# Retention attention and a snake MLP on one Trainium2 core: blocks of one batch each with a ninth block of all ends, 64x64 state products, DMA turns, and another order for the first three blocks

## The chip, the cores and the metric

The kernel runs on one core of a Trainium2 chip. The metric is device time in microseconds: three timed runs gave 337.48, 338.91 and 339.41, median 338.91. Engines are called PE (TensorE), VectorE or DVE, ScalarE or ACT, POOL (GpSimd) and SP (SyncE, which issues most DMAs).

## The reference

Eight batches of eight heads, 576 tokens, head width 64. The attention has no softmax: scores are weighted with a decay by distance.

```
scores = (q @ k^T) / 8
ret    = scores * gamma[h] ** (i - j)   for i >= j, else 0
x      = (ret @ v) with heads side by side            # 4608 tokens x 512
h      = x @ w_in                                      # 512 -> 2048
g      = h + sin(alpha * h) ** 2 / (alpha + 1e-9)
out    = g @ w_out                                     # 2048 -> 512
```

## The kernel before

The 4608 tokens are projected in nine blocks of 512. For each block `gemm1(n, fc)` makes 16 products of four 128x512 matmuls (line 385) into a PSUM bank `hps`, ScalarE takes the sine (390), one of three engines squares it (399, 401), and VectorE adds h and the scaled square (406) into `gT`. `gemm2(n, u)` makes the second projection in 16 parts of four matmuls (421), four parts to a 128-token output `ops`, which ScalarE evicts (427) and SP stores (429). The projections take their input from `xT`, a ring of 2048 tokens; since a batch has 576 tokens and a block 512, a block straddles batches.

A batch's attention works on three parts: p = 0 and 1 are 256 tokens each, p = 2 the last 64 (the *ends*). Loads (110, 117) bring 512 KB per part and name; `cast` multiplies keys and queries with the decay, in two instructions of 512 elements (129), and copies values (149, 151); the operands are then *turned* (transposed), on PE by 64x64 products (206) with a copy back by ScalarE or VectorE (217, 219), or by a DMA (`crossed`, 183). `scores` multiplies keys and queries in 64x64 products (286), VectorE masks them (297). `outer` makes key-value sums of 128 tokens (231); `chain` on POOL (257, 269, 270), or for the first two batches VectorE (252), sums them up with decay into `state`, which holds each 64x64 state twice, half of it zeros, so that `add_states` can use full 128x128 products (352) on top of `values` (340). The sum goes to `xT` (363).

Each engine runs its own instructions in program order, and the order is written by hand: a prologue that computes batch 0 with filler matmuls (`keep_busy`, 455) in between, block 0's first projection, a stretch with batch 1 and half of block 0's second projection, then a loop over blocks in which lists (`at_unit`) place the next batch's attention between the 16 units of a block. A small DMA that reads w_out (`gate`, 517) holds back batch 1's loads until that slab has landed. Batches 0 to 3 are turned on PE, the others by DMA. PSUM has two double banks `mm`, three banks `hp` and one `op`.

Of the kernel before, what the change touches and what calls it, by code (L numbers as in the profile page):

```python
# [16 lines left out]
def kernel(  # L17
# [9 lines left out]
):  # L27
    nc = tc.nc
# [4 lines left out]
    P = 128  # L33
# [25 lines left out]
    ident_np = np.tile(np.eye(64, dtype=np.float16), (2, 1))  # L62

    ident_dram = nc.inline_tensor(ident_np, name="rt_ident")
# [8 lines left out]
    ident = const.tile([P, 64], F16, tag="ident", bufs=1)  # L73
# [3 lines left out]
    fac_s = {"k": cn[:, 32:36], "q": cn[:, 36:40]}  # L77
    g1 = cn[:, 40:44]
    g2 = cn[:, 44:52].rearrange("p (a t) -> p a t", t=2)
# [6 lines left out]
    RING = 2048  # L86
    xT = const.tile([P, KT, RING], F16, tag="xT", bufs=1)

    src = {"q": q, "k": k, "v": v}
    w_in_r = moe_w_in.rearrange("(Q t e d) f -> Q t d e f", Q=2, t=2, e=2)  # L90
    w_out_r = moe_w_out.rearrange("(a p) d -> p a d", p=P)

    def load_w_in(g):
        cols = slice(g * FF // 2, (g + 1) * FF // 2)
        for Q in range(2):
            for t in range(2):
                nc.gpsimd.dma_start(
                    w_in16[64 * t : 64 * t + 64, 2 * Q : 2 * Q + 2, cols], w_in_r[Q, t, :, :, cols]
                )
# [3 lines left out]

    raw = {}
    half = {}

    def load(b, nm, p):
        if p < 2:
            t_ = work.tile([P, H, 2 * D], F32, tag="raw", bufs=6, name=nm + "32")
            nc.sync.dma_start(  # L110
                t_, src[nm][b, :, 256 * p : 256 * p + 256, :].rearrange("h (i r) d -> i h (r d)", r=2)
            )
        else:
            t_ = work.tile([P, 4, D], F32, tag="raws", bufs=3, name=nm + "s32")
            view = src[nm][b, :, 512:576, :].rearrange("(hp e) i d -> e i hp d", e=2)
            for e in range(2):
                nc.sync.dma_start(t_[halves(e)], view[e])  # L117
        raw[b, nm, p] = t_
# [3 lines left out]
    def cast(b, nm, p, eng):  # L122
        t_ = raw.pop((b, nm, p))
        if p < 2:
            dst = work.tile([P, H, 2, D], F16, tag=nm + "16", bufs=nbuf[nm], name=nm + "16")
            if nm in fac:
                dst = dst.rearrange("p h r d -> p (h r d)").rearrange("p (a r t d) -> p a r t d", a=4, r=2, t=2)
                for A in range(2):
                    eng.tensor_tensor(  # L129
                        dst[:, 2 * A : 2 * A + 2].rearrange("p a r t d -> p t (a r) d"),  # L130
                        t_[:, 4 * A : 4 * A + 4].rearrange("p (t a) (r d) -> p t (a r) d", t=2, r=2),
                        fac[nm][:, 8 * A : 8 * A + 8]
                        .rearrange("p (t x) -> p t x", t=2)
                        .unsqueeze(3)
                        .to_broadcast([P, 2, 4, D]),
                        MULT,
                    )
                half[b, nm, p] = dst
                return
            d_ = dst.rearrange("p h r d -> p (h r) d")  # L140
            s_ = t_.rearrange("p h (r d) -> p (h r) d", r=2)
        else:
            d_ = dst = work.tile([P, 4, D], F16, tag=nm + "s16", bufs=3, name=nm + "s16")
            s_ = t_
            f_ = fac_s[nm].unsqueeze(2).to_broadcast([P, 4, D]) if nm in fac else None
        if nm != "v":
            eng.tensor_tensor(d_, s_, f_, MULT)
        elif eng is nc.scalar:
            eng.copy(d_, s_)
        else:  # L150
            eng.tensor_copy(d_, s_)  # L151
        half[b, nm, p] = dst

    def halves(n):
        return slice(64 * n, 64 * n + 64)

    def head_of(a, t):
        return 4 * (a // 2) + 2 * t + a % 2

    class Attention:  # L160
        def __init__(self, b):
            self.b = b
            self.c0 = b * S
            self.T = {}
            self.o = {}
            self.ret = {}
            self.sc = {}
            self.state = work.tile([P, 4, 4, 2, D], F16, tag="s16", bufs=2, name="s16")
            self.kvs = work.tile([P, 4, 4, D], F32, tag="kvs", bufs=1, name="kvs")

        def new_T(self, p):
            n = 8 if p < 2 else 2
            self.T[p] = [
                work.tile([P, n, P], F16, tag=nm + ("T" if p < 2 else "Ts"), bufs=3 if p < 2 else 2, name=nm + "T")
                for nm in "kq"
            ]

        def crossed(self, p):
            self.new_T(p)
            for w, nm in enumerate("kq"):  # L180
                x = half[self.b, nm, p]
                x = x.rearrange("p a r t d -> p (a r t d)") if p < 2 else x.rearrange("p h d -> p (h d)")
                nc.sync.dma_start_transpose(self.T[p][w], x)

        def transposes(self, p, nms="kq"):
            W = 512 if p < 2 else 128
            if p not in self.T:
                self.tr = psum.tile([P, 2, 1024], F16, tag="mm", bufs=2, name="tr")
                self.new_T(p)
            tr = self.tr  # L190
            for nm in nms:
                w = "kq".index(nm) * W
                x = half[self.b, nm, p]
                todo = []
                if p < 2:
                    for a in range(4):
                        for r in range(2):
                            todo.append([(t, g, x[halves(g), a, r, t, :], w + 128 * a + 64 * r)
                                         for t in range(2) for g in range(2)])
                else:  # L200
                    for Q in range(2):
                        todo.append([(t, g, x[halves(g), 2 * Q + t, :], w + 64 * Q)
                                     for t in range(2) for g in range(2)])
                for n, four in enumerate(todo):
                    for t, g, x_, col in four:
                        nc.tensor.matmul(  # L206
                            tr[halves(t), g, col : col + 64], x_, ident[halves(g), :],
                            start=(n == 0), stop=(n == len(todo) - 1), is_transpose=True, skip_group_check=True,
                        )

        def take(self, p, nm, eng):
            W = 512 if p < 2 else 128
            w = "kq".index(nm)
            s_ = self.tr[:, :, w * W : w * W + W].rearrange("p g (x i) -> p g x i", i=64)
            d_ = self.T[p][w].rearrange("p x (g i) -> p g x i", g=2)
            if eng is nc.scalar:
                eng.copy(d_, s_)  # L217
            else:
                eng.tensor_copy(d_, s_)  # L219

        def outer(self, ps, spare=False):
            if spare:
# [4 lines left out]
            todo = [(x, a, r) for x in range(len(ps)) for a in range(4) for r in range(2)]  # L227
            for n, (x, a, r) in enumerate(todo):
                for t in range(2):
                    for g in range(2):  # L230
                        nc.tensor.matmul(
                            kv[g][halves(t), 256 * x + 64 * a : 256 * x + 64 * a + 64],
                            half[self.b, "k", ps[x]][halves(g), a, r, t, :],
                            half[self.b, "v", ps[x]][halves(g), head_of(a, t), r, :],
                            start=(n == 0), stop=(n == len(todo) - 1), skip_group_check=True,
                        )
            N = len(ps)
            if spare:
                self.kv = kv
            else:  # L240
                nc.scalar.copy(  # L241
                    self.kvs[:, 2 * ps[0] : 2 * ps[0] + 2 * N].rearrange("p (x g) a d -> p g x (a d)", g=2),
                    kv2[:, :, 0 : 256 * N].rearrange("p g (x y) -> p g x y", x=N),
                )
# [163 lines left out]
    def rows_of(G):  # L408
        b, l = divmod(G, 9)
        if l == 8:  # L410
            return out[576 * b + 512 : 576 * b + 576, :]
# [318 lines left out]
```

## Time and profile before

| what | us |
|---|---|
| median of the runs | 338.91 |
| profiled execution, first to last instruction | 335.8 |
| last matmul ends, last copy 0.59, last stores land | 331.1 to 335.8 |
| PE / DVE / ACT / POOL busy | 311.6 / 232.5 / 170.0 / 153.9 |
| units of four 128x512 matmuls done by 64.8 / by 95.6 / in all | 24 / 48 / 288 |
| PE on one batch's ends in a steady block (scores 0.16, values 0.17, states 0.11) | 0.44 |
| ScalarE: copy of 1024 elements / sine / square / output copy | 1.01 / 0.69 / 0.63 / 0.59 |
| VectorE: four sums of L252 / inva, two instructions | 0.85 / 0.42 |
| POOL: 512 elements scaled / 1024 copied / 256 elements | 1.1 / 1.12 / 0.72 |
| DMA turn, from issue to landing | 3.3 to 3.4 |
| PE at 25.50 | first product of the first projection |

Busy times overlap across engines; a modelled matmul counts past the start of the next one, so PE's pace is read from the distance of starts. In the table by stage, a stage with PE near its length is full, the others wait. In the chain of waits each piece names who set the end there.

### The profile page before, as it was taken

Reading aid. Unit: us, or ns where it says so; the run is one execution under the profiler, and the core shown is the slowest. Engines: PE = TensorE matmul, PEld = TensorE weight load, DVE = VectorE, ACT = ScalarE, POOL = GpSimd, SP = SyncE. Lnnn points to the kernel's source line nnn. Section 1 sums busy time; section 2 is a strip of 40 time slices with the busy share of each in tenths; the row PEclk is TensorE's granted clock in tenths of the full one; section 3 lists DMA queues with packets and bytes.
Section 4 is the critical chain, followed back from the end, with each engine's and each line's share of the span. In section 5 each row is a group of like instructions: output and inputs, shape, how many; then the busy total and the mean of one; then the engine's idle time right before and its main releaser. Section 6 shows DMA issues by size and latency. Waiting matters only on the chain.

```text
span 335.8 us, 8508 instructions
## 1 busy us (share of the span) xinstructions
PE 311.6 (93%) x3561; PEld 150.2 (45%) x3561; DVE 232.5 (69%) x354; ACT 170.0 (51%) x257; POOL 153.9 (46%) x175
## 2 busy tenths in 40 slices
PE   7879947799889999999999999999999999999994
PEld 2344424444445444444444544544454444444441
DVE  3745953674849976978799779878965666666600
ACT  2427935378675563555455545554564454445411
POOL 0861380694793995499149906990720000000000
PEclk9989995999999999999999999999999999999998
DMA  8999989996242768993869487947111112111142
GB/s 217 260 205 205 262 223 286 204 234 169 57 123 71 194 158 169 183 273 94 180 166 266 104 158 189 279 94 150 41 33 31 34 31 56 38 33 31 32 94 63
DMA packets 93511, 47.77 MB, mean 142 GB/s; under 512 B 36496, under 2 KB 87840, under 8 KB 93472
## 3 DMA queue, kind: packets, MB, share of 16 engines
q1 hardware_dynamic: 89712, 42.89, 54.0%
q0 software_dynamic: 3264, 4.20, 7.1%
q8 instruction: 28, 0.46, 0.6%
q10 hardware_dynamic: 496, 0.13, 0.2%
q14 instruction: 11, 0.09, 0.1%
HBM read 37.23 MB, written 9.44 MB: 139 GB/s over the span
## 4 chain that ended last, share of the span: by engine, by line
PE 66%; POOL 9%; DVE 8%; ACT 5%; DMA 5%; issue 3%; SPq 2%; ACTq 1%; POOLq 0%
PE ops L421 30%; PE hps L385 27%; DVE ret L297 3%; PE o L340 3%; POOL s L257 2%; PE o L352 2%; DMA qT<-q 2%; ACT s_t L390 2%; PE sc L286 2%; DVE gT L406 2%; DMA eye<-rt_eye 2%; SPq L117 1%; DMA k<-in_k_dram 1%; POOL kvs L270 1%; POOL k L129 1%
## 5 line engine op out<-in xcount | busy, mean ns | idle before, releaser
L390 ACT ACTIVATE s_t<-hps,alpha_t 128x512 f16<-128x512 f32 x144 | 98.6, 687 | 110.6 <-PE hps L385 106.2
L385 PE MATMUL hps<-xT,w_in 128*128 128x512 f16 x576 | 145.7, 380 | 3.6 <-DVE gT L406 2.5
L421 PE MATMUL ops<-w_out,gT 128*128 128x512 f16 x576 | 146.2, 381 | 0.0
L406 DVE SCALAR_TENSOR_TENSOR gT<-ss_t,inva,hps 128x512 f16<-128x512 f16 x144 | 106.9, 747 | 12.0 <-ACT ss_t L399 7.5
L401 DVE TENSOR_TENSOR ss_t<-s_t 128x512 f16<-128x512 f16 x124 | 71.8, 579 | 45.9 <-ACT s_t L390 45.4
L385 PEld LDWEIGHTS <-w_in 128*128 128x128 f16 x576 | 56.4, 98 | 71.7 <-issue 5.6
L421 PEld LDWEIGHTS <-gT 128*128 128x128 f16 x576 | 53.4, 98 | 60.2 <-issue 0.8
L257 POOL TENSOR_TENSOR s<-kvs,cn 128x512 f16<-128x512 f32 x32 | 35.9, 1122 | 59.8 <-ACT kvs L241 46.5
L297 DVE TENSOR_TENSOR ret<-sc,mask 128x1024 f16<-128x1024 f32 x32 | 38.5, 1219 | 9.1 <-PE sc L286 8.5
L427 ACT COPY osb<-ops 128x512 f32<-128x512 f32 x36 | 21.1, 587 | 19.4 <-PE ops L421 19.4
L129 POOL TENSOR_TENSOR q<-q,cn 128x512 f16<-128x512 f32 x26 | 28.0, 1094 | 0.0
L129 POOL TENSOR_TENSOR k<-k,cn 128x512 f16<-128x512 f32 x24 | 26.3, 1113 | 2.3 <-DMA k<-in_k_dram 2.3
L363 ACT CAST xT<-o 128x1024 f16<-128x1024 f32 x14 | 14.2, 1012 | 10.3 <-PE o L352 10.3
L151 POOL CAST v<-v 128x1024 f16<-128x1024 f32 x13 | 14.6, 1122 | 8.6 <-DMA v<-in_v_dram 8.6
L270 POOL TENSOR_TENSOR kvs<-s,kvs 128x256 f32<-128x256 f32 x19 | 14.1, 742 | 7.5 <-ACT kvs L241 6.1
L286 PE MATMUL sc<-qT,kT 64*64 64x128 f16 x512 | 12.2, 220 | 3.0 <-DVE qT L219 1.3
L455 PE MATMUL idle<-zero 128*128 128x512 f16 x40 | 13.3, 469 | 1.2 <-DVE zero L450 1.2
L340 PE MATMUL o<-ret,v 64*64 64x128 f16 x512 | 11.1, 226 | 3.0 <-issue 1.8
L217 ACT COPY kT<-tr 128x1024 f16<-128x1024 f16 (+1 forms) x12 | 9.6, 797 | 8.5 <-PE tr L206 8.4
L269 POOL TENSOR_TENSOR s<-kvs,cn 128x256 f32<-128x256 f32 x19 | 13.6, 717 | 0.0
L286 PEld LDWEIGHTS <-kT 64*64 64x64 f16 x512 | 8.7, 106 | 10.8 <-issue 10.4
L340 PEld LDWEIGHTS <-v 64*64 64x64 f16 x512 | 8.3, 111 | 8.8 <-issue 8.7
(50 smaller groups left out, 136.5 us busy)
## 6 DMA issues: line engine op xcount, KB each, us to landing
out_dram<-osb SPq DMA_DIRECT2D x72, 128.0 KB, 2.4
k<-in_k_dram SPq DMA_DIRECT2D x16, 512.0 KB, 5.8
q<-in_q_dram SPq DMA_DIRECT2D x16, 512.0 KB, 6.7
v<-in_v_dram SPq DMA_DIRECT2D x16, 512.0 KB, 7.0
w_in<-in_moe_w_in_dram POOLq DMA_DIRECT2D x8, 256.0 KB, 9.8
w_out<-in_moe_w_out_dram POOLq DMA_DIRECT2D x4, 512.0 KB, 13.9
ks<-in_k_dram SPq DMA_DIRECT2D x18, 64.0 KB, 4.3
qs<-in_q_dram SPq DMA_DIRECT2D x18, 64.0 KB, 3.4
```

The source lines that it names most:

```text
L129: eng.tensor_tensor(dst[:, 2 * A : 2 * A + 2].rearrange("p a r t d -> p t (a r) d"), t_[:, 4 * A : 4 * A + 4].rearrange("p (t a) (r d) -> ...
L257: nc.gpsimd.tensor_tensor(self.state[:, n], self.kvs[:, n].unsqueeze(2).to_broadcast([P, 4, 2, D]), g2.unsqueeze(3).to_broadcast([P, 4, 2, ...
L270: nc.gpsimd.tensor_tensor(kvs[:, n], s32, kvs[:, n], ADD)
L286: nc.tensor.matmul(sc[halves(g), t, x : x + 128], T[0][halves(t), 2 * a + r, halves(g)], T[1][halves(t), 2 * a : 2 * a + 2, halves(g)], st ...
L297: nc.vector.tensor_tensor(ret.rearrange("p t (z x) -> p (t z) x", z=2), sc.rearrange("p t (z x) -> p (t z) x", z=2), mask[:, 0:256].unsque ...
L340: nc.tensor.matmul(o[halves(t), g, N * a : N * a + N], x, y, start=(n == 0), stop=False, skip_group_check=True,)
L385: nc.tensor.matmul(hps, w_in16[:, a, fc * P : (fc + 1) * P], xT[:, a, bs0 : bs0 + 512], start=(a == 0), stop=(a == KT - 1),)
L390: nc.scalar.activation(s_t, hps, mybir.ActivationFunctionType.Sin, bias=0.0, scale=alpha_t[:, fc : fc + 1],)
L401: eng.tensor_tensor(ss_t, s_t, s_t, MULT)
L406: nc.vector.scalar_tensor_tensor(gT[n][:, fc, :], ss_t, inva[:, fc : fc + 1], hps, MULT, ADD)
L421: nc.tensor.matmul(o, gT[n][:, fk, c * P : (c + 1) * P], w_out16[:, fk, :], start=(fk == 0), stop=(fk == FC - 1),)
L427: nc.scalar.copy(osb, o)
```

## The change

Blocks 0 to 7 are now the first 512 tokens of one batch each (`xT` is a tile per batch), and block 8 holds the eight ends (`xS`): the ends of two batches share the 128 partitions in one tile, their keys and queries are turned by DMA only, and the class `Ends` computes two such pairs at once during block 7. States are stored once (`state` for three chunks, `sS` for the last of each batch), and `add_states` uses 64x64 products like the rest. `values` comes in two calls, by `same`: first the products whose row half of the array adds into the other bank of the pair, then those that add into their own, with a drain of PE (`change_rows`) between. Casts are one instruction of 1024 elements, or two halves on two engines. On PE a turn is a 128x128 product (`turn`), one operand at a time, for batches 0 and 1 alone; batches 2 and 3 now go by DMA. w_in comes in four slabs of 512 columns, w_out's first slab opens the gate.

The order of blocks 0 to 2 is new: 19 filler matmuls instead of 40; block 0's first four units and block 1's first three are done in halves of 256 tokens, the first halves ahead of the rest; batch 1 runs beside all of block 0's second projection; batch 2 is computed within block 1 and batch 3 within block 2, one block ahead as in the loop. POOL casts batches 2 and 3 during block 1.

```
-            for n, (g, x, c, a) in enumerate(todo):
-                nc.tensor.matmul(
-                    self.o[p][:, g, N * x : N * x + N],
-                    self.state[:, c, a].rearrange("p t d -> p (t d)"),
...
+    def change_rows():
+        nc.tensor.drain()
...
+        def values(self, p, same):
+            for x in range(2):
+                for r in range(2):
+                    for e in range(2):
+                        for g in range(2):
+                            t = g if same else 1 - g
...
+                            matmul(
+                                o[halves(e), t, c : c + 128],
+                                v16[halves(g), 4 * t + 2 * x + e, r, :],
+                                self.ret[p, x][halves(g), t, m : m + 128],
...
+        def add_states(self, p, gs=(0, 1)):
...
+                            matmul(
+                                o[halves(e), t, c : c + 128],
+                                st[halves(t), a, :],
+                                qT[halves(t), 2 * a : 2 * a + 2, halves(g)],
...
+    def turn(b, nm, p, ys=(0, 1), tag="hp"):
...
+                matmul(
+                    tr[:, 256 * a + 128 * r : 256 * a + 128 * r + 128],
+                    x[:, a, r].rearrange("p t d -> p (t d)"),
+                    ident,
...
-        loads(0, (0, 1, 2))
+        for nm, p in ("k0", "q0", "k1", "q1", "v0", "v1"):
+            load(0, nm, int(p))
...
-        nc.sync.dma_start(gate, w_out16[:, 4, 0:64])
-        loads(1, (0,))
-        loads(0, (2,))
-        loads(1, (1,))
+        nc.sync.dma_start(gate, w_out16[:, 0, 0:64])
+        for nm, p in ("k0", "q0", "k1", "q1", "v0", "v1"):
+            load(1, nm, int(p))
...
+        for u in range(4):
+            project(0, u, 0, TAGS[u])
...
+        firsts(0, 4, TAGS, "GVGAGVGAGVGAGVGA", 1, {
+            8: [lambda: second(0)],
+            12: [lambda: second(1)],
+            15: [lambda: second(2), lambda: refill("k", 0, V)],
+            17: [lambda: refill("q", 0, V)],
+        })
+        second(4, 5)
+        turn(1, "k", 0)
+        take(1, "k", 0, A_)
+        second(3)
+        refill("k", 1, V)
+        second(6)
+        turn(1, "q", 0)
+        take(1, "q", 0, A_)
+        refill("q", 1, G_)
+        second(7)
+        turn(1, "k", 1)
+        take(1, "k", 1, V)
+        A.scores(0, 0)
+        A.scores(0, 1)
...
+        second(11)
+        change_rows()
+        A.values(0, True)
+        A.add_states(0)
+        A.outer((1,))
...
+        firsts(1, 3, TAGS, "VAVAVAVAVAVAVAVA", 0, todo)
+        gemm2(1, 3)
+        gemm2(1, 4)
+        A.values(1, False)
+        change_rows()
+        A.values(0, True)
+        A.add_states(0)
...
+            if A:
+                at_unit(0, lambda: A.scores(0, 0), lambda: A.scores(0, 1))
...
+                at_unit(4, lambda: A.outer((0, 1)), lambda: A.scores(1, 0), lambda: A.evict((0, 1)))
+                behind(4, lambda: A.chain((0, 1, 2, 3)), lambda: A.masked(1, 0))
+                at_unit(8, lambda: A.scores(1, 1), lambda: A.values(0, False))
...
+                at_unit(12, lambda: A.values(1, False), change_rows, lambda: A.values(0, True), lambda: A.add_states(0))
...
+        for u in range(15):
+            gemm2(8, u, "hp")
+        gemm2(8, 15, "hp", slice(0, 256))
+        gemm2(8, 15, "hp", slice(256, 512))
```

`project` is `gemm1` without the sine and may do half a block; `firsts` runs a block's 16 units with sine, square (by the letter: V, A or G) and product, `lag` units apart; `second(u)` and `gemm2(n, u)` do one part of the second projection; `refill` casts a part of batch 1 and loads the same part of batch 2; `keep` copies the attention's output to `xT`.

Three places show how the instructions move. The first is VectorE from its first cast to the first block, before (numbers behind a name count tiles):

```order
L129 TENSOR_TENSOR k_121<-k_77,cn 128x2x4x64 x2
L129 TENSOR_TENSOR q_165<-q_79,cn 128x2x4x64 x2
L469 TENSOR_SCALAR inva<-al_ps 128x16
L470 RECIPROCAL inva<-inva 128x16
L129 TENSOR_TENSOR k_274<-k_83,cn 128x2x4x64 x2
L297 TENSOR_TENSOR ret<-sc,mask 128x1024
L129 TENSOR_TENSOR q_334<-q_85,cn 128x2x4x64 x2
L297 TENSOR_TENSOR ret<-sc,mask 128x1024
L252 SCALAR_TENSOR_TENSOR kvs<-kvs,cn,kv 128x64 x4
```

and now:

```order
L161 TENSOR_TENSOR k_113<-k_78,cn 128x2x8x64
L161 TENSOR_TENSOR q_132<-q_80,cn 128x2x8x64
L161 TENSOR_TENSOR k_145<-k_82,cn 128x2x4x64
L307 TENSOR_TENSOR ret<-sc,mask 128x1024
L161 TENSOR_TENSOR q_200<-q_84,cn 128x2x4x64
L307 TENSOR_TENSOR ret<-sc,mask 128x1024 x3
L269 SCALAR_TENSOR_TENSOR kvs<-kvs,cn,kv 128x64 x4
L274 TENSOR_TENSOR s_100<-kvs,cn 128x256
L562 TENSOR_SCALAR inva<-alpha_t 128x16
L563 RECIPROCAL inva<-inva 128x16
L269 SCALAR_TENSOR_TENSOR kvs<-kvs,cn,kv 128x64 x4
L274 TENSOR_TENSOR s_100<-kvs,cn 128x256
```

Half of the second key and query tiles went to POOL, inva moved behind the masks, and two states came over from POOL.

The second is SP's queue from the gate on, before:

```order
L517 DMA gate<-w_out_72 128x64
L110 DMA k_564<-in_k_dram 128x8x128
L110 DMA q_566<-in_q_dram 128x8x128
L110 DMA v_568<-in_v_dram 128x8x128
L117 DMA ks_570<-in_k_dram 64x4x64 x2
L117 DMA qs_573<-in_q_dram 64x4x64 x2
L117 DMA vs_576<-in_v_dram 64x4x64 x2
L110 DMA k_579<-in_k_dram 128x8x128
L110 DMA q_581<-in_q_dram 128x8x128
```

and now:

```order
L582 DMA gate<-w_out_72 128x64
L113 DMA k_455<-in_k_dram 128x8x128
L113 DMA q_457<-in_q_dram 128x8x128
L113 DMA k_459<-in_k_dram 128x8x128
L113 DMA q_461<-in_q_dram 128x8x128
L113 DMA v_463<-in_v_dram 128x8x128
L113 DMA v_465<-in_v_dram 128x8x128
L113 DMA k_658<-in_k_dram 128x8x128
```

The small loads of batch 0's ends no longer stand between batch 1's first and second half.

The third is POOL over the time of block 1, before (its first batch here is batch 2, whose keys are partly VectorE's):

```order
L129 TENSOR_TENSOR q_1190<-q_845,cn 128x2x4x64 x2
L151 CAST v_1274<-v_909 128x1024
L147 TENSOR_TENSOR ks_1292<-ks_1080,cn 128x256
L147 TENSOR_TENSOR qs_1294<-qs_1083,cn 128x256
L151 CAST vs_1296<-vs_1086 128x256
L129 TENSOR_TENSOR k_1298<-k_1076,cn 128x2x4x64 x2
L257 TENSOR_TENSOR s_1259<-kvs,cn 128x512
L269 TENSOR_TENSOR s_1431<-kvs,cn 128x256
```

and now:

```order
L274 TENSOR_TENSOR sS<-kvs,cn 128x256
L161 TENSOR_TENSOR k_1081<-k_658,cn 128x2x8x64
L161 TENSOR_TENSOR q_1094<-q_666,cn 128x2x8x64
L161 TENSOR_TENSOR k_1111<-k_698,cn 128x2x8x64
L161 TENSOR_TENSOR q_1125<-q_717,cn 128x2x8x64
L104 CAST v_1143<-v_776 128x1024
L104 CAST v_1162<-v_861 128x1024
L161 TENSOR_TENSOR k_1176<-k_1083,cn 128x2x8x64
```

The pairs of 512-element casts became single instructions of 1024, twelve casts of two batches stand in a row, and the state chain of batch 2 follows behind them.

## Rows read from the trace of the kernel before

**Rows 1.** The page's first line: the profiled execution.
```profile
span 335.8 us, 8508 instructions
```

**Rows 2.** Table by stage: stretch, length, each engine's busy time, granted clock, DMA.
```profile
0.00:25.50 25.50, 19.35 (x373) 9.57 (x374) 12.75 (x28) 8.95 (x11) 13.43 (x21) 0.95 1.05 227
25.50:64.80 39.30, 30.63 (x465) 15.79 (x464) 25.75 (x42) 23.83 (x37) 14.85 (x15) 0.90 1.06 237
64.80:95.60 30.80, 28.29 (x464) 13.78 (x464) 18.86 (x27) 21.68 (x35) 23.70 (x28) 1.00 0.56 143
95.60:335.80 240.20, 233.33 (x2260) 111.05 (x2259) 175.09 (x257) 115.57 (x175) 101.88 (x113) 1.00 0.51 118
```

**Rows 3.** Timeline of PE, 198 to 231 us: start, length, instruction, count.
```profile
198.42 0.64 PE L286 MATMUL sc<-qT,kT 64*64 64x128 f16 x32 [0.29 <-DMA qT<-q]
...
220.05 1.03 PE L421 MATMUL ops<-w_out,gT 128*128 128x512 f16 x4
...
229.54 1.03 PE L385 MATMUL hps<-xT,w_in 128*128 128x512 f16 x4
230.50 0.64 PE L286 MATMUL sc<-qT,kT 64*64 64x128 f16 x32
```

**Rows 4.** Chain of waits, 0 to 70 us: start, length, what set the end.
```profile
21.10 1.83 issue
...
37.79 1.52 SPq L117
...
43.08 4.42 DMA k<-in_k_dram
47.50 0.02 issue
47.52 2.16 DVE k L129 x2
...
62.60 0.57 PE o L340 x32
63.17 0.57 PE o L352 x8
```

**Rows 5.** Table by stage, two stretches with batch 1 (columns as in rows 2).
```profile
47.80:53.20 5.40, 1.05 (x49) 0.86 (x49) 5.35 (x6) 1.60 (x2) 2.62 (x3) 0.73 1.10 290
53.20:57.20 4.00, 4.00 (x89) 2.37 (x89) 0.00 (x0) 1.76 (x4) 0.00 (x0) 0.51 1.05 276
```

**Rows 6.** Timeline, 5 to 34 us: the first cast and three DMA issues.
```profile
5.12 1.29 DVE L129 TENSOR_TENSOR k<-k,cn 128x512 f16<-128x512 f32 x2 [3.95 <-DMA k<-in_k_dram]
6.97 1.75 SPq L110 DMA_DIRECT2D v<-in_v_dram  x1
10.01 0.78 POOL L97 DMA_DIRECT2D w_in<-in_moe_w_in_dram  x1
33.31 0.53 SPq L110 DMA_DIRECT2D k<-in_k_dram  x1
```

**Rows 7.** Those three DMAs: size, time from issue to landing.
```profile
v<-in_v_dram SPq DMA_DIRECT2D x1, 512.0 KB, 7.8
w_in<-in_moe_w_in_dram POOLq DMA_DIRECT2D x1, 256.0 KB, 7.5
k<-in_k_dram SPq DMA_DIRECT2D x1, 512.0 KB, 6.3
```

**Rows 8.** Instructions by form: all, 264 to 317, 181 to 192 us; busy, mean ns.
```profile
L297 DVE TENSOR_TENSOR ret<-sc,mask 128x1024 f16<-128x1024 f32 x32 | 38.5, 1219 | 9.1 <-PE sc L286 8.5
...
L406 DVE SCALAR_TENSOR_TENSOR gT<-ss_t,inva,hps 128x512 f16<-128x512 f16 x31 | 23.2, 748 | 1.2
L401 DVE TENSOR_TENSOR ss_t<-s_t 128x512 f16<-128x512 f16 x30 | 12.8, 425 | 15.4 <-ACT s_t L390 15.4
...
L401 DVE TENSOR_TENSOR ss_t<-s_t 128x512 f16<-128x512 f16 x6 | 5.3, 877 | 2.2 <-ACT s_t L390 2.0
```

**Rows 9.** Timeline, 181 to 183 us: a square beside POOL's key cast.
```profile
181.13 2.22 POOL L129 TENSOR_TENSOR k<-k,cn 128x512 f16<-128x512 f32 x2
...
181.12 1.32 DVE L401 TENSOR_TENSOR ss_t<-s_t 128x512 f16<-128x512 f16 x1
```

More of the change, by code (lines that the diff above doesn't have):

```diff
@@ new lines, in values @@
+        def values(self, w, same):
+            if w not in self.o:
+                self.o[w] = psum.tile([P, 2, 512], F32, tag="mm", bufs=2, name="os")
+            o, v16 = self.o[w], half[2 * self.js[w], "v", 2]
+            for x in range(2):
+                for e in range(2):
+                    for g in range(2):
+                        t = g if same else 1 - g
+                        c = 128 * x + 64 * g
+                        matmul(
+                            o[halves(e), t, c : c + 64],
+                            v16[halves(g), 4 * t + 2 * x + e, :],
+                            self.ret[halves(g), t, w, 2 * x + e, :],
+                            start=(not same and x == 0), stop=False, skip_group_check=True,
+                        )
@@ L416, in gemm2, with finish @@
+    def finish(n, c, cols, eng=None):
+        osb = work.tile([P, 512], F32, tag="osb", bufs=4, name="osb")
+        copy(eng or nc.scalar, osb[:, cols], ops[n, c][:, cols])
+        for h in range(2):
+            nc.sync.dma_start(rows_of(n, c, h)[:, cols], osb[halves(h), cols])
+    def gemm2(n, u, tag="op", cols=slice(0, 512), end=True):
         c, part = divmod(u, 4)
-        if part == 0:
-            ops[n, c] = psum.tile([P, 512], F32, tag=bank, bufs=1 if bank == "op" else 3, name="ops")
@@ L469 @@
[L469 to L486 removed]
+        turn(0, "q", 0)
@@ new lines @@
+        cast(0, "v", 0, A_)
+        keep_busy(2)
+        A.scores(1, 0)
+        A.masked(1, 0)
+        A.outer((0,), spare=True)
+        A.scores(1, 1)
+        A.first_sum(A_)
+        A.to_state(0)
+        A.masked(1, 1)
+        cast(0, "v", 1, G_)
+        load_w_in(3)
+        for g in range(4):
+            load_w_out(g)
+        A.next_sum(1)
+        A.to_state(1, V)
+        nc.vector.tensor_scalar_add(inva, alpha_t, 1e-9)
+        nc.vector.reciprocal(inva, inva)
+        A.values(0, False)
@@ new lines @@
+        second(4, 5)
[10 more added lines that the diff above has]
+        take(1, "k", 1, V)
+        A.scores(0, 0)
+        A.scores(0, 1)
+        A.masked(0, 0)
+        refill("v", 0, A_)
+        second(8)
+        turn(1, "q", 1)
+        take(1, "q", 1, A_)
+        A.masked(0, 1)
+        second(9)
@@ L487 @@
+        A.outer((0,))
+        A.scores(1, 0)
+        A.first_sum(A_)
         A.to_state(0)
+        A.masked(1, 0)
         A.next_sum(1)
         A.to_state(1)
-        keep_busy(4)
-        A.transposes(1, "q")
-        A.take(1, "q", A_)
-        cast(0, "v", 1, A_)
-        keep_busy(2)
-        A.values(0)
-        A.scores_pe(1, 0)
-        A.scores_mask(1, 0)
-        A.outer((1,), spare=True)
+        refill("v", 1, A_)
+        second(10)
+        A.values(0, False)
+        A.scores(1, 1)
@@ L580 @@
-        A.outer((1,), spare=True)
-        A.next_sum(2)
-        A.to_state(2)
-        more()
-        A.scores(1, 1)
-        A0.scores_small()
-        A.next_sum(3)
-        A.to_state(3)
-        cast(2, "q", 0, G_)
-        more()
-        A0.values(2)
-        A0.add_states(2)
-        A.values(1)
-        A.add_states(1)
-        load(2, "v", 1)
-        for n in range(1, NBLK + 1):
-            A1, A = A, Attention(2) if n == 1 else A2
-            todo = {}
+        second(12)
+        second(13)
```

808 lines of the change are left out of this document (386 added, 422 removed).

## The prediction

> **What bounds the kernel now.** Read the span first, then the stretches. The profiled execution spans 335.8 us [rows 1] against a median of 338.91 us of the three timed runs: 3.1 us lie around the span, and I add them at the end. The table by stage [rows 2] shows where to look: from 95.6 us on TensorE (PE) is busy 233 of 240 us, and in 25.5 to 64.8 us only 30.6 of 39.3. Call four 128x512 matmuls of one accumulation a unit; the two projections are 2 x 9 x 16 = 288 units. The pace is in [rows 3]: eleven units lie between the starts at 220.05 and 229.54, 0.863 us each, and one block of 32 units with one batch's attention lasts 230.50 - 198.42 = 32.1 us, of which 32.1 - 32 x 0.865 = 4.4 are attention. So 240 units with five batches account for nearly all that follows 95.6 us: 240 x 0.865 = 207.6, and 32.6 remain. The slack lies ahead of it. By 64.8 us 24 units (20.8 us of work) are done, by 95.6 us 48.
>
> What holds the early stages, by the chain of waits [rows 4]: SyncE issues the twelve small loads of the ends up to 43 us, behind them the second key tile takes 4.42 us to land, VectorE needs 2.16 us to scale it, and PE stands. That costs twice: in 47.8 to 53.2 us PE works 1.05 of 5.4 us, and in the 4 us behind it, where it is busy throughout, the granted clock is 0.51, the 1.2 GHz level [rows 5].
>
> **Start.** The change drops 21 of 40 filler matmuls, puts the loads in the order k, q, k, q, v, v and moves the ends' loads to blocks 2 to 5. The first load is there at 5.12, the sixth at 6.97 + 7.8 = 14.8 [rows 6, 7], so 1.9 us each: k1 at 9.0 instead of 10.7, v0 at 12.7 instead of 9.0. VectorE then works nearly without a gap, as before: keys 1.29, queries to 8.5, half a key tile beside POOL (1.03) to 10.0. The first mask now waits for the turn of k1, which stands ahead of the scores on PE: 11.5. Mask 1.22, half a query tile 0.69, mask: 14.6. The last queries' turn, the copy of 1.01 and the scores put the third mask at 15.4 to 16.6, the fourth at 16.9 to 18.1; sums 0.85, state 0.37, inva 0.42, sums 0.85, state 0.37 end at 21.0, PE's states at 21.2. The first half products (they need only the first 256 tokens) follow at once, where before the first product starts at 25.5. I add 1 us for PE's lower clock with fewer fillers: 22.2. w_in is no later: its first half megabyte lands at 10.0 + 7.5 = 17.5 [rows 6, 7], the new slab of 1 MB is two such pieces, about 19.
>
> **Block 0.** PE has 16 units of the first projection and three of the second: four half units 1.7, then 4 x 0.43 + 12 x 0.865 + 3 x 0.865 = 14.7. With 2 us for a cold start (4 us at half rate, as in [rows 5]) it ends at 40.6. VectorE has 16 products at 0.748 and four squares at about 0.6, since eight moved to POOL, and scales k0 (1.3) in between: 15.7 from 28.2, so 43.9. That is no earlier than before.
>
> **Batch 1.** The gain is here, and it is the order. The same six loads stand directly behind the gate. Before, the first is issued at 33.31 and lands 6.3 later [rows 6, 7], at 39.6; at 1.9 each the others come by 41.5, 43.4, 45.3, 47.2, 49.1 at the latest. From 43.9 the walk is: q0 scaled 45.3; on PE units 3 and 6 of the second projection (they wait for the last product), then the turn to 46.2; ScalarE copies q0 and evicts to 47.9, which frees the bank for the turn of k1; turn, copy, scores, first mask 50.7, second 52.0; q1 copied 52.2; outer product and scores 52.8; third mask 54.0, sums 54.9, and only these free the bank that the first values need: 55.3; fourth mask 56.8; values and states 57.2, copy 58.2, second outer product 58.7, sums and state 60.0; meanwhile two units and three half units, second values and states 62.9, two units: 64.6. Every wait of 0.3 to 1 us is covered by a unit of the second projection or shows as PE idle; none is like that of [rows 5], so I leave the clock at its 2.4 GHz level. At 64.6 us 33.5 units are done, where before 24 are: 9.5 x 0.865 = 8.2 us.
>
> **Block 1.** PE's own need is small (14.5 units and three of the second projection 15.1, attention 2.2), VectorE bounds: 16 products 12.0, four masks 4.9 and eight squares. POOL scales two batches here without a pause, and that has a price. The square that starts with POOL's cast at 181.12 lasts 1.32 [rows 9] instead of 0.425; in 181 to 192 us, with POOL full, the six last 0.877 on average [rows 8]. Eight at 0.877 are 7.0. From 1.2 behind 64.6, 23.9 us: 89.7. Then two units, the rest of batch 2's attention 1.6, two units: 94.8, with 55 units done. The Trainium skill (SBUF — State Buffer, section Who interferes with whom) says that a VectorE instruction with two SBUF inputs and a POOL instruction that reads SBUF exclude each other for a whole instruction; the trace agrees: that square ends at 182.4, just behind the first of POOL's two instructions, which fill 2.22. By that rule the change, which merges two POOL instructions of 512 elements into one of 1024, doubles the wait; the rival below has its price.
>
> **The rest.** 233 units: 201.5. A batch's attention costs now 4.41 a block, 0.44 of it for the ends: 3.97. The states cost 0.57 for eight full-array products, 32 quadrant products of the same width also 0.57 [rows 4]; so 12 at 0.06 to 0.07 become 24 at 0.018, some 0.28 less, and the added drain gives it back. A drain isn't in the trace. Below, nothing; above, the 1.83 us for which PE stood at 21.10 with no releaser [rows 4]. I take 0.25, near a matmul's own 0.22 plus a weight load, because the other waits of PE are that short. Five batches at 3.94: 19.7. The ends, now four pairs at once, 2.8 with two drains. Block 2 has 25 units, 25.6 with the attention, and 24.7 us of VectorE work (16 products, 12 squares at 0.6, four masks, a copy): 1 us lost. Tail 4.7 as before. Sum 94.8 + 201.5 + 19.7 + 2.8 + 1 + 4.7 = 324.5; the stages after 95.6 save some 4 us because batch 3 and the ends no longer turn on PE. The DMA turns for batches 2 and 3 are hidden: q(2) is scaled at 66.2, lands 3.3 later, and its scores come at unit 8, about 73; without that cover each us late is one us on PE. With the 3.1 around the span: 327.6, the forecast.
>
> **Rivals.** *Longer lock.* If merged casts double a square's wait (0.45 more each), block 1 loses 3.6 and block 2, whose VectorE has only 0.9 to spare, 12 x 0.45 = 5.4 less that, 4.5: 335.7. Blocks 3 to 6 hold it, since VectorE has over 5 us of 32 free there. For: the square ends behind a POOL instruction's end. Against: the products between squares use up part of the wait. *Weights side by side.* If the larger slabs share the DMA engines instead of going in turn, w_out's first slab comes about 4 us later than its first use, where PE then stands, and the gate holds batch 1's loads 1.5 us more: 333. Against: one w_in piece lands 7.5 after its issue while the others queue. *Drains.* Slower: if each of the twelve drains empties PE's queue and costs the 1.83 us of that bare wait, 12 x 1.58 = 19 us are added: 346.6. It decides from 1.2 us per drain, where the 11.3 us gained are gone. For: no cover stands behind a drain, PE being the bound. Against: at the many semaphore waits of PE nothing like it shows; the 1.83 us occur once, with DMA full.
>
> **Chances.** Forecast (317 to 333) 0.70, weights 0.10, lock 0.12, drains 0.08. Half a per cent, what a measurement of this kernel can tell from no change, is 1.7 us: 337.2 to 340.6. The forecast is faster throughout; of weights 0.09 are faster and 0.01 same; of lock 0.07 and 0.05; drains slower. Faster 0.86, same 0.06, slower 0.08. The range, 317 to 337, ends below where neither cold clock (3 us) nor waiting squares (3.6) nor the short waits of batch 1 (about 3) cost anything, and above with the lock; it leaves out the drains and a tenth besides.
>
> **What would show it.** First product of the first projection near 22 us, at a granted clock of half for some us; no PE gap over 3 us between 40 and 65; block 1's last product on VectorE near 90 us; squares there of 0.9 and not 1.3 us; units of 0.865 from 95 us on with about 4 us of attention per block; PE standing less than 0.5 us at each drain. Wrong if the second batch's casts wait for DMA past 46 us, if scores of batch 2 wait for their turns, or if blocks 3 to 6 last over 33 us.

## The result, and the profile after

The changed kernel takes 326.99 us (median of 4 runs, 325.17 to 328.31) against 338.80 of the kernel before on the same chip: ratio 0.9653 (95% interval 0.9610 to 0.9696). The forecast was 327.6. The profiled execution spans 323.1 us [rows 1: 335.8], and 2.1 us lie around it. It was the fastest of the four.

By stage (same columns as [rows 2]: length, busy time of PE, its weight loads, VectorE, ScalarE and POOL, granted clock, DMA share, GB/s):

```profile
16.00:21.00 5.00, 3.09 (x122) 2.52 (x122) 4.56 (x13) 1.73 (x3) 3.47 (x5) 0.50 1.24 207
21.00:26.00 5.00, 4.73 (x61) 3.38 (x61) 1.89 (x7) 0.58 (x1) 2.47 (x4) 0.50 1.18 180
42.00:62.00 20.00, 17.74 (x308) 10.04 (x307) 14.51 (x24) 8.46 (x11) 7.11 (x6) 1.00 0.89 252
62.00:93.00 31.00, 24.07 (x310) 11.57 (x309) 22.76 (x29) 18.94 (x29) 23.25 (x21) 1.00 1.10 225
```

Batch 1's stretch, where PE did 1.05 us in 5.4 and then ran at the 1.2 GHz level [rows 5], is now 89% full at a granted clock of 1.00. Left over are a cold stretch ahead of block 0 and PE's 7 idle microseconds in block 1.

The timeline of PE (start, duration, line, output <- inputs, shape, count, and in brackets the wait before) at the points that the forecast names: the last values of batch 0, the first half product, the second key-value sum of batch 1, the first units after 33.5 units, the third scores of batch 2, the first units after 55 units:

```profile
21.19 1.36 PE L327 MATMUL o<-ret,v 64*64 64x128 f16 x30 [1.28 <-issue]
...
22.91 1.46 PE L447 MATMUL hps<-xT,w_in 128*128 128x256 f16 x6
...
55.73 0.43 PE L247 MATMUL kv<-v,k 64*64 64x64 f16 x32
...
62.05 1.15 PE L447 MATMUL hps<-xT,w_in 128*128 128x256 f16 x9
...
77.94 0.42 PE L296 MATMUL sc<-qT,kT 64*64 64x128 f16 x16 [1.58 <-DVE gT L471]
...
92.80 1.03 PE L447 MATMUL hps<-xT,w_in 128*128 128x512 f16 x4
```

At 92.80 us 55 units are done, where before 48 were at 95.6. The seven units are worth 6.05 us, so 8.85 of the 12.7 us of span are gained by here.

VectorE, POOL and the turn of k1 in batch 1 (same timeline, all engines):

```profile
43.55 1.21 DVE L161 TENSOR_TENSOR q<-q,cn 128x1024 f16<-128x1024 f32 x1
...
44.24 2.29 POOL L161 TENSOR_TENSOR q<-q,cn 128x1024 f16<-128x1024 f32 x1 [3.01 <-PE ops L491]
...
44.69 2.92 DVE L161 TENSOR_TENSOR k<-k,cn 128x1024 f16<-128x1024 f32 x1
...
47.66 0.62 PE L194 MATMUL tr<-ident,k 128*128 128x128 f16 x8 [1.35 <-DVE k L161]
```

The key cast takes 2.92 us where the query cast just before took 1.21. It ends at 47.61, 1.08 behind POOL's cast (46.53), so nearly its whole work lies behind that. The timeline of block 1 shows such a pair of a square and a cast, and VectorE's last product there:

```profile
79.87 1.90 POOL L161 TENSOR_TENSOR q<-q,cn 128x1024 f16<-128x1024 f32 x1 [3.10 <-DMA q<-in_q_dram]
80.08 1.97 DVE L466 TENSOR_TENSOR ss_t<-s_t 128x512 f16<-128x512 f16 x1 [1.50 <-ACT s_t L455]
...
86.82 0.75 DVE L471 SCALAR_TENSOR_TENSOR gT<-ss_t,inva,hps 128x512 f16<-128x512 f16 x1
```

A steady block, answering to [rows 3]: PE's timeline from unit 12's first projection to its second; the drain stands among the 32 values of the second row:

```profile
174.47 1.03 PE L447 MATMUL hps<-xT,w_in 128*128 128x512 f16 x4
175.42 0.93 PE L327 MATMUL o<-ret,v 64*64 64x128 f16 x32
176.18 0.29 PE L345 MATMUL o<-qT,s 64*64 64x128 f16 x8
176.29 0.40 PE L327 MATMUL o<-ret,v 64*64 64x128 f16 x16
176.51 0.40 PE L345 MATMUL o<-qT,s 64*64 64x128 f16 x16
176.84 1.04 PE L491 MATMUL ops<-w_out,gT 128*128 128x512 f16 x4
```

The 16 values of the fourth row last 0.22 us to the next row, the 32 of the second, with the drain, 0.76: the drain is some 0.32. A block lasts 31.55 us (before 32.1).

### The profile page after: what moved, and what is told of

The parts are those of the page before. It is cut to its first block, busy times and chain, and to the rows that moved or that the text cites. A ratio compares the mean times of both kernels' runs of the same rounds, so it can differ in the third digit from the quotient of the medians.

```text
span 323.1 us, 7702 instructions
## 1 busy us (share of the span) xinstructions
PE 299.7 (93%) x3188; PEld 146.1 (45%) x3188; DVE 218.9 (68%) x321; ACT 171.1 (53%) x262; POOL 135.5 (42%) x137
## 4 chain that ended last, share of the span: by engine, by line
PE 75%; DVE 13%; issue 3%; ACT 2%; POOL 2%; DMA 2%; SPq 0%; ACTq 0%; POOLq 0%; DVEq 0%
PE ops L491 34%; PE hps L447 33%; DVE gT L471 5%; DVE ss_t L466 3%; DVE ret L307 3%; PE sc L296 2%; PE o L327 2%; DMA k<-in_k_dram 2%; PE kv L247 2%; DVE k L161 1%; POOL k L161 1%; ACT s_t L455 1%; PE o L345 1%; PE tr L194 1%; POOL q L161 1%
## 5 line engine op out<-in xcount | busy, mean ns | idle before, releaser
L447 PE MATMUL hps<-xT,w_in 128*128 128x512 f16 (+1 forms) x540 | 129.4, 372 | 1.5 <-DVE gT L471 1.5
L447 PEld LDWEIGHTS <-w_in 128*128 128x128 f16 x604 | 59.0, 99 | 67.7 <-issue 2.6
L466 DVE TENSOR_TENSOR ss_t<-s_t 128x512 f16<-128x512 f16 x96 | 57.2, 595 | 23.7 <-ACT s_t L455 23.6
L274 POOL TENSOR_TENSOR s<-kvs,cn 128x256 f16<-128x256 f32 x21 | 13.3, 635 | 63.8 <-ACT kvs L102 61.6
L102 ACT COPY osb<-ops 128x512 f32<-128x512 f32 (+1 forms) x37 | 21.3, 574 | 19.3 <-PE ops L491 16.3
L161 POOL TENSOR_TENSOR q<-q,cn 128x1024 f16<-128x1024 f32 (+1 forms) x14 | 26.7, 1906 | 8.3 <-DMA q<-in_q_dram 5.3
L161 POOL TENSOR_TENSOR k<-k,cn 128x1024 f16<-128x1024 f32 (+1 forms) x13 | 25.7, 1975 | 8.6 <-DMA k<-in_k_dram 8.6
L464 ACT ACTIVATE ss_t<-s_t 128x512 f16<-128x512 f16 x40 | 25.3, 632 | 0.3
L102 ACT CAST xT<-o 128x1024 f16<-128x1024 f32 (+1 forms) x16 | 12.8, 799 | 13.6 <-DVE xT L104 9.1
L447 PE MATMUL hps<-xS,w_in 128*128 128x512 f16 x64 | 16.4, 379 | 0.0
L466 POOL TENSOR_TENSOR ss_t<-s_t 128x512 f16<-128x512 f16 x8 | 8.5, 1064 | 7.6 <-ACT s_t L455 6.3
```

The costliest lines, as they stand in the source:

```text
L161: eng.tensor_tensor(dst[:, a0:a1].rearrange("p a r t d -> p t (a r) d"), t_.rearrange("p (t a) x -> p t a x", t=2)[:, :, a0:a1].rearrange( ...
L447: matmul(hps_of[n, fc][0][:, cols], w_in16[:, a, fc * P : (fc + 1) * P], xs[n][:, a, cols], start=(a == 0 and part != 1), stop=(a == KT - ...
L464: nc.scalar.activation(ss_t, s_t, mybir.ActivationFunctionType.Square)
L466: eng.tensor_tensor(ss_t, s_t, s_t, MULT)
```

## The experiments

VectorE's 144 products and ScalarE's 144 sines are all in each trace, so the distance between the n-th of them in two traces compares stages. "End" is the end of a block's last product, all in us of the profiled execution:

| kernel | first product | end of block 0 | to block 1's first sine | to end of block 1 | to block 2's first sine | to end of block 2 | rest | median of the runs |
|---|---|---|---|---|---|---|---|---|
| after | 22.9 | 43.6 | 19.1 | 24.8 | 6.3 | 27.7 | 201.5 | 326.99 |
| after, again | 23.8 | 43.9 | 19.1 | 23.9 | 9.0 | 27.6 | 201.5 | 325.53 |
| ends early | 23.2 | 43.9 | 19.3 | 24.7 | 6.3 | 27.7 | 201.6 | 327.41 |
| squares on ScalarE | 23.0 | 44.2 | 19.1 | 25.1 | 9.0 | 27.7 | 202.0 | 327.92 |
| casts split | 23.5 | 44.6 | 18.8 | 23.0 | 6.6 | 26.7 | 201.2 | 323.09 |
| fillers | 22.9 | 42.9 | 17.6 | 23.3 | 8.1 | 27.7 | 201.6 | 323.87 |
| q1 on VectorE | 23.2 | 44.3 | 17.7 | 23.0 | 6.7 | 27.7 | 201.5 | 324.80 |
| whole units | 24.2 | 44.6 | 17.8 | 22.2 | 9.0 | 27.7 | 201.5 | 324.82 |
| joined | 23.1 | 43.0 | 17.7 | 23.0 | 7.9 | 26.7 | 201.3 | 321.97 |

What follows block 2 is the same to 0.3 us but for the squares kernel (0.4) and the split casts (-0.3): runs differ ahead of it. The kernel after gave 325.2 to 328.3 in one group and 321.8 to 327.5 in another, so a median of one edit alone says little below 1%, and I read the stages. Edits 5 to 8 also ran on another chip than 1 to 4 and 9 to 11, without the kernel after beside them; the kernel before took 338.38 us there against 339.61 and 339.42. By their medians 6, 7 and 8 come to 0.957 to 0.960 of the kernel before, the kernel after in its second group to 0.958: no gain of one of these three shows in its time.

**1. The ends' loads early again** (kernel after)
```
-        for nm, p in ("k0", "q0", "k1", "q1", "v0", "v1"):
+        for nm, p in ("k0", "q0"):
             load(1, nm, int(p))
+        for nm in "kqv":
+            load(0, nm, 2); load(1, nm, 2)
+        for nm, p in ("k1", "q1", "v0", "v1"): ...
```


> The kernel after, with the six loads of batch 0's and 1's ends put back between batch 1's first two loads and the other four (in block 2 their loads go). Theory (the order of the loads carries the gain of batch 1): SyncE's issues of the ends took 5.3 us before, and 0.75 MB at 1.9 us per 0.5 MB is 2.9 us of transfer, so k1, q1, v0, v1 land 3 to 5 us later; v0, which is copied 8.8 us behind its issue, and v1 are then late: 329 to 332 us. Rival (the loads were hidden anyway, the order of the computation alone gained): 327, within 1.


Measured 327.41 (325.45 to 328.64): the rival. k1 is issued at 41.49 instead of 30.55 and VectorE waits for it, by the timeline:
```profile
46.22 1.23 DVE L161 TENSOR_TENSOR k<-k,cn 128x1024 f16<-128x1024 f32 x1 [1.18 <-DMA k<-in_k_dram]
...
48.14 1.90 POOL L161 TENSOR_TENSOR q<-q,cn 128x1024 f16<-128x1024 f32 x1 [6.63 <-PE tr L194]
```
But now POOL's cast comes after it, so it takes 1.23 and ends at 47.45, no later than the 47.61 of the kernel after. The late load cost nothing because the wait for POOL that it replaced was as long. In the joined kernel (10) the key cast starts at 44.09, ahead of such a load; no run shows whether the order of the loads counts there.

**2. The order of the loads alone** (kernel before)
```
         loads(1, (0,))
-        loads(0, (2,))
         loads(1, (1,))
+        loads(0, (2,))
```


> The kernel before, with one edit: the ends' loads of batch 0 stand behind all six of batch 1's. Theory: k1 is issued 5.3 us earlier, so most of PE's wait in 47.8 to 53.2 us goes and the clock stays up; the ends are late instead, but stand behind k1's turn: 334 to 337 us instead of 338.8. Rival (the gain needs the new walk of batch 1): the ends take k1's place as the late operand, 338 to 340.


Measured 333.92 against 339.61 (ratio 0.9835, 0.9788 to 0.9881): 5.7 us, a little more than expected. The two stretches of [rows 5], by stage:
```profile
47.80:53.20 5.40, 2.42 (x108) 1.39 (x100) 3.01 (x4) 2.06 (x4) 1.51 (x3) 1.00 0.72 165
53.20:57.20 4.00, 3.32 (x100) 1.80 (x94) 1.21 (x2) 2.87 (x3) 3.41 (x5) 1.00 1.10 309
```
PE works more than twice as long in the first, and the clock no longer falls in the second. By the medians, moving six small loads is nearly half of the whole gain. The two traces show only 2.4 us of it (spans 335.8 and 333.3): that of the kernel before lies 3.1 us under its median of 338.91, this one 0.6 under its own. So its size lies somewhere from 2.4 to 5.7 us; block 1's first sine comes 2.6 earlier (63.26 instead of 65.89).

**3. 64 more drains**
```
                 project(n, u)
+                if 3 <= n < 7:
+                    change_rows()
```


> The kernel after, with 64 more drains of PE, one behind each first-projection unit of blocks 3 to 6. Theory (a drain costs 0.15 to 0.25 us, a pipeline's length): 9.6 to 16 us more, 336.6 to 343. Rival of the forecast (1.83 us each, a bare wait of PE's queue): 64 x 1.83 = 117 more, 444. A drain that is free: 327.


Measured 345.12, above the range. The rest behind block 2 is 220.7 instead of 201.5: 19.2 / 64 = 0.30 us each. PE's timeline with them, a drain behind each L447 row:
```profile
177.03 1.03 PE L447 MATMUL hps<-xT,w_in 128*128 128x512 f16 x4
178.16 1.03 PE L491 MATMUL ops<-w_out,gT 128*128 128x512 f16 x4
179.03 1.03 PE L447 MATMUL hps<-xT,w_in 128*128 128x512 f16 x4
```
1.13 from projection to the next row, 0.87 for the unit without a drain. That is 0.27 for a drain here, and 0.30 on average. The rival of 1.83 us is out; both are a little over the range I gave.

**4. Four of block 1's squares moved to ScalarE**
```
-        firsts(1, 3, TAGS, "VAVAVAVAVAVAVAVA", 0, todo)
+        firsts(1, 3, TAGS, "AVAAAVAAAVAAAVAA", 0, todo)
```


> The kernel after, with 12 instead of 8 of block 1's squares on ScalarE, so 4 on VectorE. Theory (VectorE bounds block 1): it sheds 4 x 0.825 = 3.3 us, and the start of block 2 comes 2 to 3.3 us earlier than 92.8: 323.7 to 325 us. Rival (ScalarE with 16 x 0.69 + 12 x 0.63 + copies = 22 us, or PE's waits on attention, bound it just as closely): 326.5 to 328.


Measured 327.92; block 1's stretch is 25.1, not shorter. VectorE's four squares take 1.06 to 1.94 us, each beside POOL, and a product waits 3 us for ScalarE (timeline):
```profile
64.68 0.75 DVE L471 SCALAR_TENSOR_TENSOR gT<-ss_t,inva,hps 128x512 f16<-128x512 f16 x1 [3.01 <-ACT ss_t L464]
...
65.35 1.94 DVE L466 TENSOR_TENSOR ss_t<-s_t 128x512 f16<-128x512 f16 x1
...
70.03 1.33 DVE L466 TENSOR_TENSOR ss_t<-s_t 128x512 f16<-128x512 f16 x1
```
In all VectorE waits 5.5 us there for ScalarE's squares, in the kernel after not at all. So VectorE's work alone doesn't bound block 1: with four squares less it waits for ScalarE's sine and square instead.

**5. POOL's casts in two instructions**
```
+            if eng is nc.gpsimd and len(ys) == 2:
+                cast(b, nm, p, eng, (0,)); cast(b, nm, p, eng, (1,)); return
```


> The kernel after, with POOL's casts of keys and queries again in two instructions of 512 elements. Theory (the merged casts do not lengthen the waits, part of which lies under the products): POOL's casts take 2.2 instead of 1.9 us, VectorE's eight squares in block 1 stay near 0.8 us: 326.2 to 327.8 us. Rival (a square waits for a whole POOL instruction, so the merged cast doubles the wait): squares there fall to 0.6, block 1 and block 2 shorten by 2 to 4 us together: 323 to 325.


Measured 323.09 (ratio 0.9545, 0.9514 to 0.9576), the rival's time. Block 1's eight squares average 0.67 instead of 0.82 us and block 2's 0.57 instead of 0.76; block 2 is 1.0 us shorter, the rest 0.3. These 1.2 us are shown: every kernel with merged casts has 27.6 or 27.7 for block 2, and this one and the joined one 26.7. Block 1's 23.0 instead of 24.8 is not: with merged casts the drains kernel (3) and 7 have 23.0 there too, and 8 has 22.2.

**6. 20 more fillers** in the prologue
```
-        keep_busy(2)   # ahead of scores(0, 0); the others likewise
+        keep_busy(6)
```


> The kernel after, with 20 more filler matmuls of 512 columns in the prologue (39 instead of 19). Theory (VectorE sets the end of block 0, so the 1.2 GHz level in 16 to 26 us is covered): granted clock 1.00 there if PE is kept at work, PE through block 0 up to 2 us earlier, VectorE's last product of block 0 within 0.7 us of 43.6: 326 to 327.5 us. Rival (the slow stretch is on the path): 323.5 to 325. If the fillers stand in the way of scores: 328 to 330.


Measured 323.87, the rival's time. The clock is 1.00 in 16 to 26 us, and VectorE's last product of block 0 comes at 42.9, within the 0.7 expected. But the larger part of what its trace gains up to block 1 is not the clock: by the timeline the pair of casts fell the other way round,
```profile
43.95 1.21 DVE L161 TENSOR_TENSOR k<-k,cn 128x1024 f16<-128x1024 f32 x1
...
44.60 2.32 POOL L161 TENSOR_TENSOR q<-q,cn 128x1024 f16<-128x1024 f32 x1 [4.11 <-DMA q<-in_q_dram]
```
VectorE first, and now POOL waits. Batch 1's stretch is 17.6 instead of 19.1.

**7. Batch 1's second query tile on VectorE**
```
-        refill("q", 1, G_)
+        refill("q", 1, V)
```


> The kernel after, with batch 1's second query tile scaled by VectorE behind the key tile instead of by POOL beside it. Theory (the key cast took 2.92 us instead of 1.3 because POOL's cast ran beside it): the key cast falls to 1.2 to 1.4, its turn starts 1.3 us or more earlier than 47.66, and VectorE gives about half back: 325.5 to 326.5 us. Rival (it was the transfers of that time): the cast stays at 2.5 to 3 and VectorE gets 1.3 more: 328.


Measured 324.80; the key cast, now with nothing beside it, takes 1.21, and its turn starts at 46.82 although block 0 ended 0.7 later (timeline):
```profile
45.37 1.21 DVE L161 TENSOR_TENSOR k<-k,cn 128x1024 f16<-128x1024 f32 x1
...
46.50 1.21 DVE L161 TENSOR_TENSOR q<-q,cn 128x1024 f16<-128x1024 f32 x1
...
46.82 0.61 PE L194 MATMUL tr<-ident,k 128*128 128x128 f16 x8
```
17.7 instead of 19.1: the wait for POOL costs batch 1 1.4 us, transfers have no part in it, and VectorE gives nothing back in this stretch.

**8. Whole units** in blocks 0 and 1
```
-        for u in range(4):
-            project(0, u, 0, TAGS[u])
-        firsts(0, 4, ...   firsts(1, 3, ...
+        firsts(0, 0, ...   firsts(1, 0, ...
```


> The kernel after, with the first units of blocks 0 and 1 whole instead of in halves of 256 tokens. Theory: the first product comes at 24.4 instead of 22.9, but the first sine does not come later, since it needs a whole unit: 0.5 us at most; in block 1 the three halves (1.3 us) no longer fill PE's wait for the last masks: 327.5 to 329 us. Rival (the halves' early start is worth its 1.5 us in full, and the 1.3 too): 329.5 to 330.5. Halves worth nothing: 326.5 to 327.3.


Measured 324.82, below every case. The first product and the first sine without halves, from the timeline:
```profile
24.18 6.19 PE L447 MATMUL hps<-xT,w_in 128*128 128x512 f16 x22 [0.89 <-DVE xT L104]
...
26.15 0.69 ACT L455 ACTIVATE s_t<-hps,alpha_t 128x512 f16<-128x512 f32 x1 [1.49 <-PE hps L447]
```
With halves the first sine is at 26.87: a sine needs a whole unit, and four first halves stand in front of the first second half. In block 1 the last values start at 58.48 instead of 59.22, because no halves stand ahead of them. Block 1's 22.2 instead of 24.8 is not shown to come from the whole units: in 12 they make it longer.

**9 to 11. The kernel after again, the joined edits 5, 6 and 7, and with them 16 matmuls of zeros in block 1**
```
+        def fill(m):
+            for _ in range(m):
+                matmul(ops[1, 0], zero[:, 0:P], zero, start=False, stop=False, ...)
+        for u in (6, 7, 9, 10, 12, 13, 15):
+            todo.setdefault(u, []).append(lambda u=u: fill(4 if u == 15 else 2))
```


> The kernel after, unchanged, beside the two that follow. The traces so far agree within 0.3 us from the last product of block 2 to the end (201.5 us) and differ ahead of it: block 1 takes 23 us from its first sine to its last product, or 24.8 where one square waits 1.97 us for a POOL cast, and the 5 us behind it run at the 1.2 GHz level or not. Theory (these two, and not the chip, make its runs differ): 325 to 328 us, each run at one of these steps. Rival (the chip of the second group is faster than the first by 1%, and the edits tried there gained nothing): 323 to 325 us, all runs close.

> The kernel after with three edits together: POOL's casts in two instructions, the 20 more fillers, batch 1's second query tile on VectorE. Theory (each takes away a wait of its own: the cold stretch 0.7 us, the key cast that waits for POOL 1.4, the squares in block 2 1.0): 319.5 to 321.5 us. Rival (they shorten the same wait, VectorE's): no better than the best of them, 323 to 324.

> The joined kernel with 16 matmuls of zeros added to an open sum of the second projection in block 1, behind units 6, 7, 9, 10, 12, 13 and 15, where PE waits. Theory (the 1.2 GHz level at 85 to 95 us follows PE's idle 7 of 31 us in block 1): the granted clock stays 1.00 up to block 2 in the profile, and the runs are those of the joined kernel without the drop, 319.5 to 320.5 us, closer together than its. Rival (the drop does not come from there): same spread as the joined kernel. If the fillers stand in the way of block 1's units: 16 x 0.22 = 3.5 us more.


Measured 325.53 (321.84 to 327.51), 321.97 (321.14 to 323.76) and 321.89 (320.67 to 322.87). Joined beats the kernel after by 1.1% (all but one of the six runs of the kernel after are slower than all of the joined) and the kernel before by 4.9% (ratio 0.9509, 0.9465 to 0.9554); it is a little above the range expected, and the kernel with zeros misses its own. One run of the kernel after, 321.84, lies under the range expected for it. The group ran on the first group's chip, so it doesn't settle whether the other chip is faster. The stretch behind block 1 (by stage), of the kernel after in the first execution and in this one:
```profile
84.00:97.00 13.00, 10.77 (x157) 5.15 (x157) 6.54 (x10) 5.46 (x8) 7.15 (x11) 1.00 1.14 239
84.00:97.00 13.00, 10.34 (x129) 4.68 (x128) 3.93 (x6) 4.19 (x6) 7.33 (x11) 0.74 1.17 245
```
of whole units (8) and of the joined kernel:
```profile
84.00:97.00 13.00, 11.56 (x135) 5.54 (x136) 3.88 (x6) 4.27 (x7) 6.69 (x11) 0.74 1.04 252
84.00:97.00 13.00, 12.14 (x144) 5.96 (x143) 5.21 (x7) 5.14 (x8) 6.03 (x10) 0.87 1.19 245
```
and with the matmuls of zeros:
```profile
84.00:97.00 13.00, 10.90 (x144) 5.27 (x145) 5.38 (x8) 5.02 (x8) 6.27 (x10) 1.00 1.16 242
```
The kernel after runs part of it at the 1.2 GHz level in this execution, but not in the first, where the step to block 2's first sine was 6.3 instead of 9.0 us; 4 and 8 have the same 0.74 and 9.0. With the matmuls of zeros the clock stays at 1.00, but block 1 is 0.4 us longer and the median the same. It also stayed at 1.00 without them in four traces (the kernel after's first, 1, 5 and 7). That the fall follows PE's idle time in block 1 is not shown, and the traces speak against it: between block 1's first sine and its last product PE stands 6.1 us in the kernel after's first trace, where the clock did not fall, and 3.1 us in 8, where it did. The cause stays open.

**12. Joined, with whole units**: edits 5 to 8 together.


> The joined kernel with the first units of blocks 0 and 1 whole. Theory (with halves the first sine came at 26.87 us, without them at 26.15, and in block 1 the three halves stand ahead of the last values, 0.7 us: halves gain nothing): first product 1.1 us later, the first sine of block 1 not later than 60.9, the last product of block 1 up to 0.8 us earlier: 320.8 to 322.2 us. Rival (that kernel without halves gained only from another phase against POOL's casts, and the halves' work is missed once this is settled): 2 us more than the joined kernel, 323.5 to 324.5.


Measured 321.71 (on a third chip), stages 43.1, 16.8, 24.0, 7.6, 26.7, 201.3 in the table's order. The first sine of block 1 is 0.9 us earlier and block 1 1.0 longer: no gain of the halves shows.

## Why the prediction was right, and where its parts were not

The forecast held within 0.6 us of the median and 1.4 of the span, and most of the gain lies where it said: 11 of the 12.7 us of span are there by the end of batch 1's stretch. But "it is the order" is shown for the loads in the kernel before (2) alone; in the new kernel their old order cost nothing (1), and the order of the work was not tried by itself. The parts were less exact than the sum.

**Start and block 0.** First product 22.9 (22.2 said), VectorE's last product 43.6 (43.9). The last values of batch 0 waited 1.28 us with no releaser in the trace, which I hadn't foreseen. The cold stretch is there, worth 0.7 to 1.7 us by experiment 6 (block 0's end at 42.9 against 43.6 to 44.6), since VectorE covers part. That an earlier first product helps at all was wrong: the first sine does not come earlier for it (8).

**Batch 1.** 62.05 us instead of 64.6, so the term was too large by 2.5. (What held the second key tile back before were six small loads, not twelve, as the queue of the kernel before shows.) My walk put the second key-value sum behind the copy of the first values, ending at 58.7; in the program it stands ahead of that copy and ran at 55.73. Against it stands a wait I had not priced, 1.4 us of the key cast behind POOL's cast. The bound on the gain from the order of the loads was sound (2), but in the new program the same loads are not on the path (1): there VectorE's key cast waits for POOL as long. At 62.05 us the new kernel is 11 us ahead of the old one at 64.8 (2.75 us and 9.5 units). What is left of them beyond the 2.4 to 5.7 us of the loads comes from the new start and walk together, which no run here took apart further.

**Block 1.** 25.5 us from 62.05 to its last product, 25.1 said, the squares 0.82 against 0.877. The reason given was too narrow: VectorE is not the only bound (4).

**Longer lock.** I gave it 0.12 and 8.1 us. It is real and smaller: splitting the casts back gains 1.2 us, 1.0 of them in block 2, where I had priced 4.5; block 2's squares lose 0.2 us each to the merged casts and not 0.45 (5). In block 1, priced at 3.6, no loss of time is shown. The rule of the Trainium skill (SBUF — State Buffer, section Who interferes with whom) that such pairs exclude each other for a whole instruction is borne out by each pair shown: 44.69 with 2.92, 80.08 with 1.97, and the other way round in 6. I misjudged how often a square meets a cast; that is a matter of phase: the square that took 1.97 us at 80.08 takes 0.43 in 3, 6 and 7, and the POOL cast that it met had itself waited for a load.

**Rest.** 230.3 from 92.8 us on, 229.7 said. Attention in a steady block is 31.55 - 32 x 0.865 = 3.87 (3.94); the ends cost 30.65 - 27.62 = 3.0 in block 7 (2.8). A drain costs 0.27 to 0.30 between full products and 0.32 in its place (0.25); the estimate by the nearest short waits was good, the bare wait of 1.83 us was something else.

**What was missed.** Against the plan batch 1 is 2.5 us short, block 1 0.4 long, the way to the 55th unit 0.1 and the rest 0.6; that makes the span 1.4 us shorter. What is added around the span is 0.8 larger: 326.99 - 323.1 = 3.9 instead of 3.1. So one error of 2.5 us is met by four small ones of the other sign, and that 0.6 remain is luck. Of the 3.9 us, 1.8 are what the profiled execution lies under the median; that the clock behind block 1, which fell in 4, 8 and 9 and cost up to 2.7 us, makes up this part is likely, but only one of the four runs was traced.

Of the other rivals, the larger weights did no harm: the gate was issued at 28.40 us, where the kernel before has 32.67, and PE never waited for w_out. One sign of being wrong came true in part. Batch 2's turns were not hidden throughout, against what I said: PE stood 1.58 us ahead of the third scores (77.94), released by a turn's landing and a product at nearly the same time; no run here separates the two.

## What to carry over

Look first for the load that lands last in a stretch where the engine stands: moving it ahead of loads not yet needed was worth 5.7 us of the median (2.4 of the traced span) with nothing else changed. In the new kernel the same move was worth nothing, because another wait was as long. Keep long casts of VectorE and POOL off each other on the path: put both on one engine, or split them. Before computing halves, ask whether a consumer can use a half product; here the sine could not.

## What was not expected of the hardware

A VectorE cast of 1024 elements takes 1.21 us alone and 2.92 when POOL's started 0.45 us earlier; if VectorE starts first, POOL's takes 2.32 instead of 1.90. A drain of PE between full products costs 0.27 to 0.30 us. With the same program the granted clock in 84 to 97 us was 1.00 in one execution and 0.74 in another, though PE had stood 6.1 us of block 1 in the former and 5.0 in the latter.
